# A 160-byte unused tile behind the constants and a decay tile 64 bytes longer: every later tile moves in SBUF

## The chip, the cores and the metric

The kernel runs on one core of one Trainium2 chip. The metric is the device time of one execution in microseconds. Three executions of the kernel before took 225.80 (median), 225.74 and 226.55 us. A profiled execution took 225.21 us, and 223.5 us of it lie between the first and the last instruction of the program (the span). The changes looked at here are small, so every sum below is made against that one profiled execution and then carried over to the median.

## What is computed

The reference has two parts. The first is a Mamba-2 state scan over x (4 batches, 8 heads, 768 steps, 32 channels) with decays a and projections B and C of 16 states, in chunks:

```
log_a = np.log(np.clip(a, 1e-06, 1.0))
...
    cum = np.cumsum(la, axis=-1)
    L = np.exp(cum[:, :, :, None] - cum[:, :, None, :])
...
    M = CB * L
    y_intra = np.einsum('bhij,bhjd->bhid', M, xc)
    decay_to_i = np.exp(cum)
    y_inter = np.einsum('bhin,bhnd->bhid', Cc, state) * decay_to_i[:, :, :, None]
    y[:, :, sl] = y_intra + y_inter
...
    state = decay_full[:, :, None, None] * state + np.sum(Bx, axis=2)
```

The second is a mixer on that result, seen as 4 x 768 tokens of 256 channels: a low-rank mix over the tokens (rank 32), and a two-layer network over the channels (256 to 1024 and back):

```
h = xt @ U @ V
u = x + h.transpose(0, 2, 1)
ch = np.maximum(u @ w_ch1, 0.0) @ w_ch2
return (u + ch).astype(np.float32)
```

Everything is in 32-bit floating point at the interface; four of the weights arrive as 64-bit words and are converted on the chip.

## The kernel before

**Stages.** Each batch is worked in three pairs of 128-step blocks (`pairs`, twelve in all). For a pair the scan loads B, C and x, multiplies in the decays (`prep`, `decayed`), transposes (`turning`), forms the chunk matrices (`gram`, `mask`), updates the states (`state`, `update`) and adds up the output (`inter`, `intra`, `yout`). Then the mixer of that batch does the low-rank part (`project`, `mixed`, `added`) and, for three blocks of 256 tokens, the two layers.

**The two layers.** The first blocks go through `plain`, with 32-bit weights (`w1f`, and `w2f` in tiles named `o`). All other blocks use products in the replicated format FP32R. Each operand is split into a near part, a far part and a joined part, and three products take the place of one. The weights are split once, in `refine`, into the three tiles `w1[0..2]` (printed as w10, w11, w12) and `w2[0..2]`. The inputs of the first layer are split in `split` into three tiles `u0`, `u1`, `u2`; the outputs of the first layer are split in `second` and `third` into tiles named `words`. All products come from the one line in `products` (L772):

```
nc.tensor.matmul(out=t, lhsT=lhsT, rhs=rhs, start=start, stop=True,
                 skip_group_check=True)
```

`lhsT` is the stationary operand (128 columns, 512 B a partition), which a weight load brings in; `rhs` is the moving operand (256 columns, 1024 B a partition). Three uses of it matter here:

- the **up** products (`first` and `second`): stationary w1, moving u; in the profile `x<-u,w` and `z<-u,w`, 480 of them
- the **down** products (`down`): stationary w2, moving words; `x<-words,w` and `z<-words,w`, 432 of them
- the products of **the last block** (`rows`): the roles are exchanged, stationary words, moving w2; `x<-w,words` and `z<-w,words`, 48 of them

**What sets the order.** The order of the work is written out by hand as a list of steps (`PLANS`), and `follow` runs through it; no scheduler moves anything. All instructions of an engine stand in that order. SyncE's queue issues all loads and stores.

**What sets the addresses.** Tiles are laid out in each partition one after the other, pool by pool, each rounded up to 32 B: the pool `const` first (weights, identity, decay constants; the last of it is `settled`, one number), then `raw` (the loads bc and x, and twelve tiles `words`), then `att` (the tiles of the scan: BC, T, Cm, `own`, bd, M, S, Sm, in this order), then `mix` (yT, ytok, pT, o, u0, u1, u2). `own` is a temporary of `keep`, which runs once, at the start, for the decays of the chunks. In the kernel before it has 4 x 11 x 8 numbers, 1408 B.

Of the kernel before, what the change touches and what calls it, by code (L numbers as in the profile page):

```python
# [10 lines left out]
FP32 = mybir.dt.float32  # L11
# [63 lines left out]
def kernel(  # L75
# [28 lines left out]
    P = 128  # L104
    NB, NH, S, D = x.shape
# [13 lines left out]
    Q = 32  # L119
# [3 lines left out]
    const = ctx.enter_context(tc.tile_pool(name="const", bufs=1))  # L123
    raw = ctx.enter_context(tc.tile_pool(name="raw", bufs=4))
    att = ctx.enter_context(tc.tile_pool(name="att", bufs=2))
# [17 lines left out]
    def bank(tag, *dims):  # L143
        t = psum.tile([P, *dims], FP32, tag=tag, name=tag, bufs=BANKS[tag])
        if fills[0]:
            idle(t if len(dims) == 1 else t.rearrange(
                {2: "p a b -> p (a b)", 3: "p a b c -> p (a b c)"}[len(dims)]), fills[0])
        fills[0] = 0
        return t
# [101 lines left out]
    own = {}  # L251
# [124 lines left out]
    def keep(bs, tag="w"):  # L376

        n = bs.stop - bs.start
        d = bank(tag, n, NC, NH)
        nc.tensor.matmul(out=d, lhsT=after, rhs=la[:, bs], start=True, stop=False,  # L380
                         skip_group_check=True)
        nc.tensor.matmul(out=d[:, :, :NC - 1], lhsT=onward, rhs=la[:, bs, 1:], start=False,
                         stop=True, skip_group_check=True)
        nc.scalar.activation(FD[:, bs], d, AF.Exp)

        d = bank(tag, n, NC, 2, NH)
        nc.tensor.matmul(out=d[:, :, :, 0], lhsT=middle, rhs=la[:, bs], start=True, stop=True,
                         skip_group_check=True)
        for m, sl in ((high, slice(0, NC - 1)), (low[0], slice(1, NC))):
            nc.tensor.matmul(out=d[:, :, :NC - 1, 1], lhsT=m, rhs=la[:, bs, sl], start=False,  # L390
                             stop=True, skip_group_check=True)
        J = 2 * NC - 1
        own = att.tile([P, NB, J, NH], FP32, tag="own", name="own", bufs=1)[:, :n]
        vector.tensor_tensor(
            out=own, in0=d.rearrange("p b c v h -> p b (c v) h")[:, :, :J],
            in1=mine[:, None, None, :].to_broadcast(own.shape), op=ALU.mult)
        vector.tensor_reduce(out=kept[:, bs], in_=own, axis=mybir.AxisListType.X, op=ALU.add)
        nc.scalar.activation(kept[:, bs], kept[:, bs], AF.Exp)
# [56 lines left out]

    st = {}
    settled = const.tile([P, 1], FP32)
    behind = {"turn": 0, "first": []}
    yT, ytok = {}, {}

    def prep(k, c=0, n=2):

        b, q = pairs[k]
        if "BC" not in st.setdefault(k, {}):
            st[k]["BC"] = att.tile([P, 2, 2, NH, N], FP32, tag="BC", name="BC")
        for g in [slice(4) if n == 2 else slice(c, c + 1) if c < 2 else slice(2, 4)]:
            part = st[k]["BC"].rearrange("p i c h n -> p (i c) h n")[:, g]
            vector.tensor_tensor(
                out=part, in0=bc_sb[k].rearrange("p h i c n -> p (i c) h n")[:, g],
                in1=F[:, b, q].rearrange("p h i c -> p (i c) h")[:, g, :, None].to_broadcast(  # L470
                    part.shape), op=ALU.mult)
# [479 lines left out]
    def ytokens_of(k, v):  # L951
# [4 lines left out]
                 j=crossed, y=yout, t=ytokens, L=load, Q=lambda k, c: prep(k, c, 1),  # L956
                 E=lambda k, c: decayed(k, c, 1), O=ytokens_of,
                 V=lambda k, c, v: turn(k, c, 1, "wx"[v // 2], vector if v % 2 else None))
    whole = dict(c=convert, R=refined, A=lambda i: decays(every_batch, "w", [i]),
                 K=lambda n: keep(every_batch, "z"), F=fill,  # L960
                 v=lambda n: spread())

# [53 lines left out]
```

## Time and profile before

| | |
|---|---|
| median of three executions | 225.80 us (225.74 to 226.55) |
| profiled execution | 225.21 us |
| its span | 223.5 us |
| granted TensorE clock | 0.999 |
| TensorE matmul busy | 214.7 us, 96% of the span |
| TensorE weight loads busy | 192.8 us, 86% |
| VectorE busy | 163.7 us, 73% |
| ScalarE busy | 122.5 us, 55% |

A matmul's busy time runs from its start to its modelled end and overlaps with the next one, so the time that a matmul costs in a dense stream isn't its duration but the distance from its start to the start of the next. That distance is called the spacing below. In the timeline view, where equal instructions in a row are merged, it can be read as the difference between the starts of two lines divided by the count of the first.

### The profile page before, as it was taken

How to read it: one execution, taken by the hardware profiler on the slowest of the kernel's cores; microseconds unless marked ns; L12 is line 12 of the kernel's file. 1: busy time of each engine (PE TensorE's matmuls, PEld its weight loads, DVE VectorE, ACT ScalarE, POOL GpSimd, SP SyncE). 2: the span in 40 equal slices, each digit the busy share in tenths (PEclk: the TensorE clock that was granted, in tenths of full speed). 3: DMA queues.
4: the chain of work that ended last, by engine and by line, in shares of the span. 5: the costliest groups of instructions: out<-in, count | busy, mean ns of one | idle time of the engine just before them, and what ended most of it. 6: DMA issues, size and time to landing. Idle time of an engine off the chain costs nothing.

```text
span 223.5 us, 7716 instructions
## 1 busy us (share of the span) xinstructions
PE 214.7 (96%) x3374; PEld 192.8 (86%) x3374; DVE 163.7 (73%) x341; ACT 122.5 (55%) x275; POOL 6.5 (3%) x22
## 2 busy tenths in 40 slices
PE   7977899899999999999999999999999999999994
PEld 5846567678889988989999997899998999999994
DVE  3489899999997979688189748948881694917541
ACT  2335774879548655674675351678332357545431
POOL 4023000000000000000000000000000000000000
PEclk9999999999999999999999999999999999999999
DMA  5977899989850005032015010200000000000142
GB/s 86 130 124 130 157 153 229 236 218 154 113 78 4 0 3 94 3 66 81 6 23 73 3 47 3 100 3 1 3 0 3 3 0 0 4 0 0 50 141 94
DMA packets 69345, 14.61 MB, mean 65 GB/s; under 512 B 63616, under 2 KB 67520, under 8 KB 69312
## 3 DMA queue, kind: packets, MB, share of 16 engines
q1 hardware_dynamic: 69312, 14.13, 32.5%
q8 instruction: 26, 0.43, 0.8%
q14 instruction: 7, 0.06, 0.1%
HBM read 10.98 MB, written 3.15 MB: 63 GB/s over the span
## 4 chain that ended last, share of the span: by engine, by line
PE 84%; SPq 8%; DMA 4%; DVE 2%; issue 1%; DVEq 0%
PE x L772 36%; PE z L772 28%; SPq L195 8%; DMA words<-in_moe_w_ch_dram 2%; PE w L730 2%; PE x L652 2%; PE w L891 2%; PE x L527 2%; PE w L701 2%; PE z L676 2%; PE x L741 2%; PE x L676 2%; DMA words<-in_moe_U_dram 1%; PE w L495 1%; PE w L562 1%
## 5 line engine op out<-in xcount | busy, mean ns | idle before, releaser
L169 DVE SCALAR_TENSOR_TENSOR words<-words 128x512 fp32r<-128x512 f32 (+6 forms) x60 | 39.5, 673 | 8.8 <-PE x L772 4.3
L772 PE MATMUL x<-words,w 128*128 128x256 f32 x288 | 39.5, 282 | 0.0
L772 PEld LDWEIGHTS x<-words,w 128*128 128x128 f32 x288 | 35.9, 188 | 1.0 <-issue 0.8
L772 PE MATMUL z<-u,w 128*128 128x256 f32 x240 | 34.4, 282 | 0.0
L772 PE MATMUL x<-u,w 128*128 128x256 f32 x240 | 33.9, 283 | 0.0
L772 PEld LDWEIGHTS z<-u,w 128*128 128x128 f32 x240 | 30.5, 188 | 0.5 <-issue 0.2
L772 PEld LDWEIGHTS x<-u,w 128*128 128x128 f32 x240 | 30.4, 189 | 0.4 <-issue 0.2
L777 ACT ACTIVATE z<-z 128x512 f32<-128x512 f32 (+1 forms) x24 | 13.7, 572 | 15.8 <-PE z L772 15.6
L777 ACT ACTIVATE x<-x 128x512 f32<-128x512 f32 (+1 forms) x27 | 15.3, 572 | 10.4 <-PE x L772 10.3
L772 PE MATMUL z<-words,w 128*128 128x256 f32 x144 | 19.5, 282 | 0.0
L772 PEld LDWEIGHTS z<-words,w 128*128 128x128 f32 x144 | 17.8, 188 | 0.3 <-issue 0.2
L169 DVE SCALAR_TENSOR_TENSOR words<-x,words 128x512 fp32r<-128x512 f32 x20 | 13.7, 686 | 4.8 <-ACT words L812 4.7
L169 DVE SCALAR_TENSOR_TENSOR words<-z,words 128x512 fp32r<-128x512 f32 x20 | 13.7, 686 | 3.1 <-ACT words L812 3.1
L812 ACT ACTIVATE words<-x 128x512 fp32r<-128x512 f32 x20 | 11.9, 600 | 6.5 <-PE x L772 6.5
L812 ACT ACTIVATE words<-z 128x512 fp32r<-128x512 f32 x20 | 11.8, 597 | 5.1 <-PE z L772 5.0
L594 ACT ACTIVATE Sm<-S,slot 128x128 f32<-128x128 f32 (+1 forms) x18 | 6.1, 389 | 14.4 <-DVE S L169 14.4
L169 DVE SCALAR_TENSOR_TENSOR S<-S,kept,w 128x64 f32<-128x64 f32 x40 | 11.2, 280 | 2.5 <-PE w L562 0.8
L169 DVE TENSOR_TENSOR BC<-bc,F 128x512 f32<-128x512 f32 (+2 forms) x18 | 8.7, 509 | 3.2 <-ACT F L372 2.6
L169 DVE TENSOR_TENSOR yT<-x,yT 128x384 f32<-128x384 f32 (+1 forms) x15 | 9.2, 616 | 2.3 <-PE x L772 2.0
L169 DVE TENSOR_TENSOR M<-x,causal 128x256 int32<-128x256 int32 x24 | 9.0, 418 | 2.4 <-PE z L527 2.4
L169 DVE TENSOR_TENSOR u<-yT,u 128x512 fp32r<-128x512 f32 x10 | 6.9, 688 | 5.2 <-ACT u L766 5.2
L652 PE MATMUL z<-T,Sm 32*64 32x64 f32 x180 | 9.7, 236 | 0.3 <-DVE settled L169 0.3
(146 smaller groups left out, 390.6 us busy)
## 6 DMA issues: line engine op xcount, KB each, us to landing
words<-in_moe_w_ch_dram SPq DMA_DIRECT2D x7, 512.0 KB, 6.0
x<-in_x_dram SPq DMA_DIRECT2D x24, 128.0 KB, 3.4
out_dram<-o SPq DMA_DIRECT2D x8, 256.0 KB, 2.2
bc<-in_B_dram SPq DMA_DIRECT2D x24, 64.0 KB, 3.4
bc<-in_C_dram SPq DMA_DIRECT2D x12, 128.0 KB, 3.3
out_dram<-words SPq DMA_DIRECT2D x3, 256.0 KB, 2.6
words<-in_moe_w_ch_dram SPq DMA_DIRECT2D x2, 256.0 KB, 4.5
out_dram<-o SPq DMA_DIRECT2D x2, 128.0 KB, 1.7
```

What stands on the lines that cost most here:

```text
L169: self.last = call(*args, **kwargs)
L195: op = nc.sync.dma_start(**kwargs)
L527: nc.tensor.matmul(out=g[r][cols, c], lhsT=s["T"][rows, 0, c, cols], rhs=s["Cm"][rows, :, :, ts(2 * c + p, Q)].rearrange("r v t i -> r v i ...
L594: nc.scalar.activation(s["Sm"][:, sl, v], s["S"][:, sl, ts(v, D)], AF.Copy, scale=slot[:, v, None])
L652: product = nc.tensor.matmul(out=y[r // 2][p][ts(r % 2, H), c], lhsT=own[ts(r, Q)], rhs=s["T"][ts(r, Q), 1, :, ts(2 * c + p, Q)].rearrange ...
L676: product = nc.tensor.matmul(out=y[n][p][ts(i, Q), c], lhsT=x_sb[k][half, c, h], rhs=s["M"][half, h // 2, c, h % 2], start=fresh(k, n, p, ...
L701: nc.tensor.transpose(out=t[:, c, g], in_=yT[b][:, g, ts(2 * q + c, P)], identity=ident)
L730: nc.tensor.matmul(out=p[ts(q, Q)], lhsT=U_sb[:, c], rhs=ytok[b][:, c, ts(q // 2, P)], start=(c == 0), stop=(c == NC - 1), skip_group_chec ...
L741: nc.tensor.matmul(out=h[q][:, :VS], lhsT=pT[rows], rhs=V4[rows], start=True, stop=True, skip_group_check=True)
L772: nc.tensor.matmul(out=t, lhsT=lhsT, rhs=rhs, start=start, stop=True, skip_group_check=True)
L777: nc.scalar.activation(t, t, AF.Copy, scale=1.0 + EPS)
L812: nc.scalar.activation(gs[j, i][0], t, AF.Relu, scale=NEAR)
```

## The change

A tile `gap` of 40 numbers (160 B) that nothing reads or writes is put behind `settled`, at the end of the pool of constants. The tile `own` becomes 368 numbers long (1472 B instead of 1408), of which the same 352 are used. No instruction is added, taken out or moved, on any engine.

```
@@ keep
         J = 2 * NC - 1
-        own = att.tile([P, NB, J, NH], FP32, tag="own", name="own", bufs=1)[:, :n]
+        own = att.tile([P, 368], FP32, tag="own", name="own", bufs=1)
+        own = own[:, :n * J * NH].rearrange("p (b j h) -> p b j h", b=n, j=J)
         vector.tensor_tensor(
...
     st = {}
     settled = const.tile([P, 1], FP32)
+    gap = const.tile([P, Q + 8], FP32)
```

So the constants stay where they are, the tiles behind them up to `own` move up by 160 B, and the tiles behind `own` by 224 B. The starts in a partition, in bytes, and what is left of them modulo 256:

| tiles | before | after | modulo 256, before | after |
|---|---|---|---|---|
| w10, w11, w12, w20, w21, w22 | 20608 and on, 8192 apart | the same | 128 | 128 |
| w1f, ident | 45184, 77952 | the same | 128 | 128 |
| bc, x, words, BC, T, Cm | words 103104 and on, 4096 apart | 103264 and on | 192 | 96 |
| bd, M, S, Sm, yT, ytok, pT, o, u0, u1, u2 | u0 213056, u1 217152, u2 221248 | u0 213280, u1 217376, u2 221472 | 64 | 32 |

The slices that the products take out of these tiles start at multiples of 256 B in them, so the table holds for every operand. With "distance" for the start of the moving operand less that of the stationary one, modulo 256:

| products | distance before | after |
|---|---|---|
| up (moving u, stationary w1) | -64 | -96 |
| down (moving words, stationary w2) | +64 | -32 |
| the last block (moving w2, stationary words) | -64 | +32 |

More of the change, by code (lines that the diff above doesn't have):

```diff
@@ L392, in keep @@
         J = 2 * NC - 1
-        own = att.tile([P, NB, J, NH], FP32, tag="own", name="own", bufs=1)[:, :n]
+        own = att.tile([P, 368], FP32, tag="own", name="own", bufs=1)
+        own = own[:, :n * J * NH].rearrange("p (b j h) -> p b j h", b=n, j=J)
         vector.tensor_tensor(
@@ L457 @@
     settled = const.tile([P, 1], FP32)
+    gap = const.tile([P, Q + 8], FP32)
     behind = {"turn": 0, "first": []}
```

## The prediction, as it was put on record before the changed kernel ran

> **What bounds the kernel now.** I read the page's first two parts, then the chain that ended last, then the waits of TensorE, and last the matmuls of line L772 in the timeline, since nothing but addresses changes and TensorE's dense stream is where an address could show.
>
> ```profile
> PE 214.7 (96%) x3374; PEld 192.8 (86%) x3374; DVE 163.7 (73%) x341; ACT 122.5 (55%) x275; POOL 6.5 (3%) x22
> ...
> PE   7977899899999999999999999999999999999994
> ...
> PE 84%; SPq 8%; DMA 4%; DVE 2%; issue 1%; DVEq 0%
> ...
> x<-in_x_dram SPq DMA_DIRECT2D x24, 128.0 KB, 3.4
> ...
> bc<-in_C_dram SPq DMA_DIRECT2D x12, 128.0 KB, 3.3
> ```
>
> TensorE's matmuls are 84% of the chain, and from the ninth slice on (45 us) its row has only nines, but for the last; the granted clock is 0.999. The waits of TensorE's matmul rows from 66 us to the end list nothing. The FP32R products begin at 67.4 us and end at 220.2 us. So in that stretch a nanosecond taken from the spacing of the products comes off the time, and one added goes onto it. Before 35 us loads and SyncE's queue lead the chain.
>
> The list of line L772's matmuls gives count and least, median and greatest duration in ns:
>
> ```profile
> L772 PE MATMUL x<-words,w x288: 276/279/388, 83.1 to 211.6; 128*128 128x256 f32 x144
> L772 PE MATMUL z<-u,w x240: 276/281/469, 67.4 to 209.7; 128*128 128x256 f32 x120
> L772 PE MATMUL x<-u,w x240: 276/281/470, 68.6 to 206.9; 128*128 128x256 f32 x120
> L772 PE MATMUL z<-words,w x144: 276/279/393, 119.2 to 213.8; 128*128 128x256 f32 x144
> L772 PE MATMUL x<-yT,w1f x32: 379/379/483, 35.6 to 52.6; 128*128 128x256 f32 x32
> ...
> L772 PE MATMUL x<-w,words x24: 276/276/369, 211.7 to 219.3; 128*128 128x256 f32 x24
> L772 PE MATMUL z<-w,words x24: 276/276/367, 216.2 to 220.2; 128*128 128x256 f32 x24
> ```
>
> All these FP32R products have the same shape. Their least duration is 276 ns everywhere, but the median is 281 for up, 279 for down and 276 for the last block. The timeline of TensorE's matmuls (start, length, operation) shows what this means for the spacing:
>
> ```profile
> 187.38 0.62 PE L772 MATMUL z<-u,w 128*128 128x256 f32 x4
> 187.84 0.62 PE L772 MATMUL x<-u,w 128*128 128x256 f32 x4
> 188.29 0.62 PE L772 MATMUL z<-u,w 128*128 128x256 f32 x4
> 188.74 1.10 PE L772 MATMUL x<-words,w 128*128 128x256 f32 x8
> 189.69 0.63 PE L772 MATMUL x<-u,w 128*128 128x256 f32 x4
> 190.16 1.11 PE L772 MATMUL x<-words,w 128*128 128x256 f32 x8
> 191.10 1.10 PE L772 MATMUL z<-u,w 128*128 128x256 f32 x8
> 192.04 1.11 PE L772 MATMUL x<-u,w 128*128 128x256 f32 x8
> ```
>
> From 187.38 to 188.74, twelve up products take 1.36 us, 113 ns each; from 190.16 to 192.04, sixteen products take 1.88 us, 117.5 each. There are two spacings, and a stream stays in one for many products. I took the starts of all consecutive FP32R matmuls out of the trace and sorted their spacings: up to 115 ns "short" (mean 113.4), 116 to 125 "long" (mean 117.8); some 30 beyond, first ones after another kind of work, are left out.
>
> - down (distance +64): 48 short, 355 long, 12% short
> - up (-64): 169 short, 285 long, 37% short
> - the last block (-64, roles exchanged): 36 short, 5 long, 88% short
> - at distance 0, where one role follows another, two cases: one short, one long
>
> The 646 long ones cost 646 x 4.4 ns = 2.85 us over an all-short stream. The mean over 900 spacings is 116.6 ns.
>
> **The change part by part.** *Instructions.* None is added, removed or moved, so no queue, wait or DMA is passed by another. The whole effect is in how long the same instructions take.
>
> *The down products' distance, +64 to -32.* No run shows -32. Its neighbours are 0 (one of two short) and -64 (37% with u moving, 88% with w2 moving). Bounds: all long, 48 x 4.4 = +0.21 us; all short, 355 x 4.4 = -1.56 us. Both neighbours are better than +64, so I take a gain; I choose the last block's 88% because its operands are the same tiles, words and w2, that the down products use: (0.88 - 0.12) x 403 x 4.4 = -1.35 us. With the up products' 37% it would be -0.44.
>
> *The up products' distance, -64 to -96.* Nothing shows -96; it is one step beyond -64, away from the bad +64. Bounds: all long, 169 x 4.4 = +0.74 us; all short, 285 x 4.4 = -1.25. From 37% I go to 50%, because a down stream that turned short would no longer hand a long rhythm to the up products behind it (at 188.74 a down group turns a short stream long, and it is long at 189.69): 0.13 x 454 x 4.4 = -0.26 us.
>
> *The last block, -64 to +32.* Between 0 and +64: half of its 36 short ones go long, 18 x 4.4 = +0.08 us (bounds -0.02 and +0.16).
>
> *A deeper stall.* The rows don't exclude that a new distance delays each product twice. At 122.2 ns (113.4 + 2 x 4.4; single spacings of 122 occur) the down products would give 355 x 4.4 + 48 x 8.8 = +2.0 us, the up products 285 x 4.4 + 169 x 8.8 = +2.7 us. I take none, and keep these for the range.
>
> *Other products.* The 32-bit ones have spacings of 215 to 216 ns both at -64 (yT, w1f) and at +128 (words, o), hence nothing; were each of the 128 to take 4.4 ns more, +0.56 us. Transposes have 108 to 110 ns at +64 (yT) and at -64 (BC), so nothing. The small products of the scan overlap, several in the array; I take nothing for them.
>
> *Loads.* The 128-byte pieces of C now straddle a multiple of 256 B, which they did not; half of x's 128-byte pieces do so before and after. x's loads land in 3.4 us, C's in 3.3 us: at most 0.1 us a load, and perhaps four of them lead work before 35 us, so 0 to 0.4 us. I take 0.
> [...]
>
> *VectorE and ScalarE.* All tiles behind the constants start at odd multiples of 32 B now, where they were multiples of 64 B. F, an operand of `prep`, already stands so. No row tells the two apart. VectorE's 27% idle time and the absence of TensorE waits after 66 us cover a few ns an instruction; a tenth more on VectorE (16 us) would not be covered and would show as TensorE waits.
>
> Sum: -1.35 - 0.26 + 0.08 = -1.5 us on the profiled 225.21. The median of the runs stands 0.6 us above it, and I put the difference on that: 225.8 - 1.5 = 224.3 us.
>
> **The rivals.** *No change.* The state of a stream would be a matter of chance after each gap, not of the distance. For this: the up products show both states on the same tiles, and both keep themselves going. Against it: 12% short at +64 and 88% in the last block. The counts would be dealt anew, within 0.8 us: 225.8.
> [...] The trace has 113.4 and 117.8 ns for the same shape at full clock, so something does delay these; what, no row here names.
>
> *Slower: the stall becomes steady, or double.* One mechanism: at the new distances the moving stream and the next weight load meet in every product. For it: at +64 this is almost so, and a stream once long stays long. Against it: no group of the trace has a steady spacing over 118. All long at one delay: 254 x 4.4 = +1.1 us, 226.9. Double for one of the two operands: 227.8 (down) or 228.5 (up); for all, 646 x 4.4 + 254 x 8.8 = +5.1, 230.9. It decides when the mean spacing passes 117.8.
>
> *All short.* Both distances lie clear of the stall: -2.85 us, 223.0.
>
> **How the numbers follow.** What a measurement of this kernel can tell from no change is about 0.5%, 1.1 us. Gain by shorter spacings 0.43 (all short 0.13 of it, forecast or near it 0.30); no change 0.25; slower 0.32, 0.13 of it beyond 228.6. Faster thus 0.43, same 0.25, slower 0.32. The likeliest case's own range is 223.0 to 224.7. For 8 in 10, the range goes from 222.9 to 228.6 (one operand doubled), leaving 0.13 above and a few hundredths below.
>
> **What would show it.** In the changed kernel's profile the rows of L772 should have a median near 276 for `words,w`, and 276 to 281 for `u,w`, and sixteen-product lines of down should stand 1.81 us apart instead of 1.88. The prediction is wrong if the medians rise above 281 or the spacing above 118 (a deeper stall), if counts are as before (no influence), or if waits of TensorE or longer VectorE rows turn up after 66 us (the alignment acts elsewhere).

## The result, and the profile after

The changed kernel took 227.95 us (median of ten executions, 226.84 to 229.65), the kernel before 225.69 (median of ten on the same chip, 224.65 to 226.88). The ratio is 1.010, 95% interval 1.007 to 1.013: the change made the kernel 1.0% slower, 2.3 us, where 1.5 us faster had been forecast. The profiled execution after took 227.66 us with a span of 225.9; before it was 225.21 and 223.5.

The page of the changed kernel, first two parts, the chain by engine, and the loads of x and C:

```profile
PE 216.1 (96%) x3374; PEld 193.8 (86%) x3374; DVE 163.8 (72%) x341; ACT 122.7 (54%) x275; POOL 6.5 (3%) x22
...
PE   7978799799999999999999999999999999999994
...
PE 88%; SPq 6%; issue 2%; DMA 1%; DVE 1%; ACT 0%; DVEq 0%
...
x<-in_x_dram SPq DMA_DIRECT2D x24, 128.0 KB, 3.9
...
bc<-in_C_dram SPq DMA_DIRECT2D x12, 128.0 KB, 4.2
```

TensorE still leads the chain. VectorE and ScalarE are busy for as long as before, to 0.2 us. Two things have moved: TensorE's matmuls are busy for 1.4 us more, and the loads land later, x in 3.9 us instead of 3.4 and C in 4.2 instead of 3.3. The matmuls of the line in `products` (L774 now), with least, median and greatest duration in ns:

```profile
L774 PE MATMUL x<-words,w x288: 276/281/388, 83.9 to 213.8; 128*128 128x256 f32 x144
L774 PE MATMUL z<-u,w x240: 277/280/468, 68.2 to 211.9; 128*128 128x256 f32 x120
...
L774 PE MATMUL x<-w,words x24: 277/280/367, 213.9 to 221.7; 128*128 128x256 f32 x24
L774 PE MATMUL z<-w,words x24: 274/280/366, 218.5 to 222.6; 128*128 128x256 f32 x24
```

The median of down went from 279 to 280 or 281, and that of the last block from 276 to 280. That of up is 1 ns lower than before and yet up has become slower, because a median says nothing of a mixture; the spacing does. The first FP32R product starts at 68.2 us instead of 67.4. In the timeline of the same kernel (start, length, operation) the long streams look like this:

```profile
192.22 1.11 PE L774 MATMUL x<-words,w 128*128 128x256 f32 x8
193.17 1.11 PE L774 MATMUL z<-u,w 128*128 128x256 f32 x8
194.12 1.11 PE L774 MATMUL x<-u,w 128*128 128x256 f32 x8
195.06 1.11 PE L774 MATMUL z<-u,w 128*128 128x256 f32 x8
196.02 1.58 PE L774 MATMUL x<-u,w 128*128 128x256 f32 x12
```

Sixteen products of up from 193.17 to 195.06 take 1.89 us, 118 ns each. One by one the spacings of up run through 115, 117, 119, 122, 120 and start again: no longer two rhythms, one of 113 and one of 118, but a single one that swings between 115 and 122. No spacing of up is 113 or 114 any more; there were 165 before. The means of the ordinary spacings (up to 126 ns; the products that come first after other work lie beyond), from the starts of all consecutive FP32R matmuls:

| products | before: distance, mean | after: distance, mean | difference |
|---|---|---|---|
| down | +64, 117.4 ns | -32, 118.2 ns | 404 x 0.9 = +0.36 us |
| up | -64, 116.1 ns | -96, 118.0 ns | 453 x 1.8 = +0.82 us |
| the last block | -64, 114.0 ns | +32, 117.0 ns | 42 x 3.0 = +0.12 us |

That is 1.3 us. With the 0.8 us by which the first FP32R product starts later, 2.1 of the 2.4 us between the two spans are accounted for. The other 0.3 us are a single wait of TensorE, in front of one small product of the scan at 144.3 us; it is the only one that the list of TensorE's waits after 66 us has (what it waited for: us in total, times, longest). For the kernel before the same list is empty:

```profile
PE z L654 <- issue: 0.3, 1, 0.3
```

A wait of 0.2 to 0.6 us in front of such a product, between 142 and 146 us, is in eight of the fourteen profiles of this case, with changed distances and with those of before. It goes neither with a distance nor with the place of the loads, and its cause is open.

### The profile page after: what moved, and what is told of

Its sections match the earlier page's. It is cut to its first block, busy times and chain, and to the rows that moved or that the text cites. A ratio compares the mean times of both kernels' runs of the same rounds, so it can differ in the third digit from the quotient of the medians.

```text
span 225.9 us, 7716 instructions
## 1 busy us (share of the span) xinstructions
PE 216.1 (96%) x3374; PEld 193.8 (86%) x3374; DVE 163.8 (72%) x341; ACT 122.7 (54%) x275; POOL 6.5 (3%) x22
## 4 chain that ended last, share of the span: by engine, by line
PE 88%; SPq 6%; issue 2%; DMA 1%; DVE 1%; ACT 0%; DVEq 0%
PE x L774 36%; PE z L774 28%; SPq L195 6%; PE x L654 3%; PE w L732 3%; PE x L529 2%; PE w L893 2%; PE z L678 2%; PE w L703 2%; PE x L678 2%; PE w L497 2%; PE x L743 1%; PE w L564 1%; DMA words<-in_moe_U_dram 1%; PE z L654 1%
## 5 line engine op out<-in xcount | busy, mean ns | idle before, releaser
L774 PE MATMUL x<-words,w 128*128 128x256 f32 x288 | 39.7, 284 | 0.0
L774 PEld LDWEIGHTS x<-words,w 128*128 128x128 f32 x288 | 36.1, 188 | 1.0 <-issue 0.8
L774 PE MATMUL z<-u,w 128*128 128x256 f32 x240 | 34.9, 284 | 0.0
L774 PE MATMUL x<-u,w 128*128 128x256 f32 x240 | 34.2, 284 | 0.0
L774 PEld LDWEIGHTS z<-u,w 128*128 128x128 f32 x240 | 30.8, 188 | 0.5 <-issue 0.2
L774 PEld LDWEIGHTS x<-u,w 128*128 128x128 f32 x240 | 30.6, 188 | 0.4 <-issue 0.2
L774 PE MATMUL z<-words,w 128*128 128x256 f32 x144 | 19.7, 283 | 0.0
L774 PEld LDWEIGHTS z<-words,w 128*128 128x128 f32 x144 | 18.0, 188 | 0.3 <-issue 0.2
```

## The experiments

Two explanations stood against each other and against chance. **A**: the distance between the moving operand and the weights, modulo 256, sets the rhythm of the FP32R products. **B**: the loads of bc and x have become slower, because their pieces now lie differently against multiples of 256 or 64 B. **C**: any move of the addresses deals the rhythm anew.

All experiments only place unused bytes: behind `settled` (as in the change), in `own`, or between x and words, where `load_v` makes a tile `skip` before the first tile `words` is made. So bc and x, words, and u can be moved apart from each other. In the diffs below, the second line that `own` needs (its rearrangement, as in the change) is left out.

One thing has to be known to read the profiles. Many executions, of the kernel before too, have a mean granted clock of 0.96 to 0.98 instead of nearly 1. In the nine profiles of this sort the clock is at about half for a while between 17 and 35 us, as in this row of the control below:

```profile
PEclk9995589999999999999999999999999999999999
```

The profiles of before, of the changed kernel and of three others (the down products alone, distance -64 for both, loads on multiples of 256 B) have no such dip. The start of the first FP32R product is therefore compared only with executions of the same sort, and the spacing after it is free of the dip. Even so that start scatters: with the loads standing as before it lies at 67.4 and 67.7 us without the dip and at 68.4 to 69.2 us with it. A difference of 0.8 us between two profiles is rough, and the ratios say more of the loads.

**The control: everything moves by 256 B.**

```
     settled = const.tile([P, 1], FP32)
+    gap = const.tile([P, 64], FP32)
```

> The unused tile is 256 B, the decay tile as before: every tile behind the constants moves, but all remainders modulo 256 and all distances are those of before. Theory A (the distance between the moving operand and the weights, modulo 256, sets the spacing of the FP32R products): mean spacing 116.6 ns as before, short ones about 12% in down, 37% in up; time within 0.5 us of before. Theory B (the loads of bc and x have become slower because their pieces lie differently against multiples of 256 or 64 B): no change either, x and C land in 3.3 to 3.4 us. Theory C (any move of the addresses deals the rhythm anew): spacing and time differ from before by up to 1 us either way.

Ratio 0.999 (0.996 to 1.002). Down 117.7, up 116.0, the last block 114.0 ns; C lands in 3.2 us. Moving by itself does nothing to the time, and explanation C falls. The counts are not fixed, though: over the six kernels with all the distances of before, down has 4 to 12% short spacings and up 29 to 44%; the control has 4% and 41%.

**The down products alone.**

```
+    gap = const.tile([P, 40], FP32)
...
-        own = att.tile([P, NB, J, NH], FP32, tag="own", name="own", bufs=1)[:, :n]
+        own = att.tile([P, 376], FP32, tag="own", name="own", bufs=1)
```

> Unused tile of 160 B, decay tile longer by 96 B: words and the loads of bc and x stand as in the changed kernel, u and everything behind the decay tile as before. Distances: down -32, up -64, the last block +32. Theory A: down 118.2 ns and the last block 117.0 as in the changed kernel, up near 116.1 as before, unless the long rhythm is handed over from down to up (then up to 117.5); in all +0.5 to +1.1 us. Theory B: the first FP32R product starts 0.8 us late (68.2 us instead of 67.4) and C lands in 4.2 us; after that no loss; +0.8 us. A and B together +1.3 to +1.9.

Ratio 1.0055 (1.003 to 1.008). Down 118.1 and the last block 117.0 ns as in the changed kernel, up 116.1 as before; C lands in 4.3 us, and the first FP32R product starts at 68.6 us, in an execution without the dip. Both A and B show, each at its place; together, 1.2 us by the ratio, they are just under the 1.3 to 1.9 that was expected.

**The up products alone.**

```
-        own = att.tile([P, NB, J, NH], FP32, tag="own", name="own", bufs=1)[:, :n]
+        own = att.tile([P, 408], FP32, tag="own", name="own", bufs=1)
```

> No unused tile, decay tile longer by 224 B: u and everything behind the decay tile stand as in the changed kernel, words and the loads of bc and x as before. Distances: up -96, down +64, the last block -64. Theory A: up near 118.0 ns, no spacing of 113 in it, +0.8 us; down 117.4 or, if no short rhythm is left to be handed over, 117.9 (+0.2). Theory B: the first FP32R product starts at 67.4 us, C lands in 3.3 us, no loss at all.

Ratio 1.003 (1.000 to 1.006). Up 117.8 ns with four spacings of 114 and none of 113; down 117.5; C lands in 3.2 us. A again. The last block went from 114.0 to 116.8 ns although its distance is that of before; it begins with a long rhythm here and keeps it longer. Why is open.

**The loads alone.**

```
+    gap = const.tile([P, 40], FP32)
...
+        raw.tile([P, 24], FP32, tag="skip", name="skip", bufs=1)
```

> Unused tile of 160 B, and a second one of 96 B between x and words: only bc and x stand as in the changed kernel, all other tiles have the remainders of before. Distances as before. Theory A: spacing as before (116.6 ns), no loss. Theory B: C lands in about 4.2 us, x in 3.9, the first FP32R product starts at about 68.2 us, the whole is 0.8 us slower.

Ratio 1.005 (1.002 to 1.008). The spacing is that of before (116.4 ns over all), and C lands in 4.2 us. B is real as well: about 1.1 us (0.4 to 1.8) with nothing else changed. The line of the load queue (packets, MB, share of the 16 engines' span), of this kernel and of the control:

```profile
q1 hardware_dynamic: 69312, 14.13, 33.0%
```

```profile
q1 hardware_dynamic: 69312, 14.13, 32.1%
```

The same packets and bytes take 0.9 points more of the span.

**Distance, or where the operands stand?** All distances after the change are odd multiples of 32 B. Here everything, the weights too, moves by 32 B, and the distances stay.

```
+    ahead = const.tile([P, 8], FP32)
     a_sb = const.tile([NB * NH * NC // 2, 2, P], FP32)
...
+    gap = const.tile([P, 56], FP32)
...
+        raw.tile([P, 8], FP32, tag="skip", name="skip", bufs=1)
```

> A tile of 32 B ahead of the constants, so weights, words and u all move by 32 B modulo 256 (weights 160, words 224, u 96), with pads that keep bc and x at their remainder of before: distances up -64, down +64, the last block -64, as before, but every operand at an odd multiple of 32 B. If the distance alone decides: means as before, up near 116, down 117.4, the last block 114, with many spacings of 113. If the operands' own alignment decides (odd multiples of 32 B lose the short state): no 113 left, up and down near 118.

Down 117.6, up 116.3, the last block 114.0 ns, with 112 spacings of 113 and 114 in up (one profiled execution; the spacings alone are read). It is the distance, not the operand's own place.

**Which boundary slows the loads?**

```
+    gap = const.tile([P, 32], FP32)
...
+        raw.tile([P, 32], FP32, tag="skip", name="skip", bufs=1)
```

> Two pads of 128 B: bc and x start at 64 modulo 256, a multiple of 64 B, all other remainders as before. The 128-byte pieces of C straddle a multiple of 256 B (they did not before), B's pieces don't, x's do in half of the cases, as before. If the straddling of 256 B is what slows the loads: C lands in about 4.2 us, and the time is up to 0.5% longer than before, as with the loads moved by 160 B. If odd multiples of 32 B are (every piece then straddles a multiple of 64 B): C lands in 3.2 to 3.3 us, and the time is as before, within 0.3%.

Ratio 1.005 (1.002 to 1.008), at a start that is a multiple of 64 B; spacing 116.6 ns as before. The loads on this page:

```profile
x<-in_x_dram SPq DMA_DIRECT2D x24, 128.0 KB, 3.8
...
bc<-in_C_dram SPq DMA_DIRECT2D x12, 128.0 KB, 4.0
```

So odd multiples of 32 B are not needed for it. What this kernel and those with the loads at 96 modulo 256 share, and the kernel before doesn't have, is that C's pieces straddle a multiple of 256 B. Over all kernels C lands in 3.1 to 3.5 us without straddling and in 4.0 to 4.3 with it.

**Distance 0.**

```
-        own = att.tile([P, NB, J, NH], FP32, tag="own", name="own", bufs=1)[:, :n]
+        own = att.tile([P, 384], FP32, tag="own", name="own", bufs=1)
...
+        raw.tile([P, 48], FP32, tag="skip", name="skip", bufs=1)
```

> bc and x as before; words and u both at 128 modulo 256: distance 0 for up, down and the last block. If distances that are multiples of 64 B keep the short state: part of the spacings at 113, mean 114 to 117.4, time from 1.0% faster to 0.3% slower. If the operands meeting at the same remainder is the worst case: all long or over, mean over 118, 0.5% slower or more.

Ratio 1.014 (1.011 to 1.017). The spacing is 119.8 ns for up and down and 119.6 for the last block, and 785 of the 900 ordinary spacings are 120. The matmuls of this kernel:

```profile
L774 PE MATMUL x<-words,w x288: 278/283/387, 84.6 to 215.4; 128*128 128x256 f32 x144
L774 PE MATMUL z<-u,w x240: 278/283/467, 68.8 to 213.6; 128*128 128x256 f32 x120
```

This is a steady stall, as the slower rival has it, with the operands starting at the same remainder; its size lies between that rival's single delay (117.8) and double delay (122.2). The 32-bit products (`yT,w1f` and `words,o`), which stand at distance 0 here too, keep their spacing of 215 to 216 ns, so in this kernel they don't show the effect.

**Distance -64 for both.**

```
-        own = att.tile([P, NB, J, NH], FP32, tag="own", name="own", bufs=1)[:, :n]
+        own = att.tile([P, 384], FP32, tag="own", name="own", bufs=1)
...
+        raw.tile([P, 32], FP32, tag="skip", name="skip", bufs=1)
```

> bc and x as before; words and u both at 64 modulo 256: distance -64 for up and down, +64 for the last block. If the distance decides, whatever the role: down becomes like up, 40% short, mean 116.1 instead of 117.4; the last block becomes like down was (117.4 instead of 114.0); up stays at 116 or gets better, as no long rhythm is handed over. In all 0.4 to 1.0 us faster, 0.2 to 0.45%. If the role matters (words against w2): down stays at 117.4, no gain.

Ratio 0.994 (0.992 to 0.997): 0.56% faster than before, a little more than the 0.2 to 0.45% expected. Down 115.0 ns with 64% short ones, where 40% had been expected, up 115.3 with 58%; the last block, now at +64, 117.8. Words behave like u at the same distance, so the role makes no difference between these two, and +64 is a long place for w2 against words too. The list of this kernel's matmuls and a piece of its timeline:

```profile
L774 PE MATMUL x<-words,w x288: 276/276/388, 83.3 to 210.6; 128*128 128x256 f32 x144
L774 PE MATMUL z<-u,w x240: 276/278/471, 67.7 to 208.7; 128*128 128x256 f32 x120
```

```profile
154.29 0.62 PE L774 MATMUL x<-u,w 128*128 128x256 f32 x4
154.75 1.98 PE L774 MATMUL x<-words,w 128*128 128x256 f32 x16
156.56 1.07 PE L774 MATMUL x<-u,w 128*128 128x256 f32 x8
```

From 154.75 to 156.56 sixteen down products take 1.81 us, 113 ns each: the rhythm that the prediction had hoped for at -32. It is not handed back and forth any more between up and down; one stretch keeps it for 101 products. Yet here, too, a long rhythm can last, in one stretch over 241 products.

**Loads on multiples of 256 B.**

```
+    gap = const.tile([P, 16], FP32)
...
+        raw.tile([P, 48], FP32, tag="skip", name="skip", bufs=1)
```

> Pads of 64 B behind the constants and 192 B between x and words: bc and x start at 0 modulo 256, all other remainders and all distances as before. No 128-byte piece of C or x straddles a multiple of 256 B any more; before, half of x's did (12,288 pieces), in the kernels with slower loads these and all of C's (24,576). If a straddling piece costs its share: x lands below 3.4 us, and the time falls by about what C's straddling added, 0.3 to 0.5%. If only C's loads stand in the way of other work: no change, within 0.2%.

Ratio 1.001 (0.998 to 1.004), x in 3.3 us, C in 3.2. No gain: that half of x's pieces straddled a multiple of 256 B before had cost nothing that can be measured, though the kernels in which C's straddle as well (96 and 64 modulo 256, distances as before) take 0.5% longer. In the profiled execution the first FP32R product starts at 65.9 us, 1.5 us before that of the kernel before, but the runs together show nothing of it.

The records of single packets say more. The pieces of C and x are 36,864 packets of 128 B. In the kernel before, 98.7% of them take at most 13 ns; with the loads alone moved it is still 93.3%, and with the loads at 64 it is 96.1%, though C's straddling pieces are a third of all. So most pieces that straddle take no longer than others; a few take far longer, up to 299 and 314 ns against 65. Straddling alone isn't the whole of B: why only some packets are drawn out, and what tells C's loads from x's, is open.

**Both together.**

```
-        own = att.tile([P, NB, J, NH], FP32, tag="own", name="own", bufs=1)[:, :n]
+        own = att.tile([P, 384], FP32, tag="own", name="own", bufs=1)
...
+    gap = const.tile([P, 16], FP32)
...
+        raw.tile([P, 16], FP32, tag="skip", name="skip", bufs=1)
```

> Both together: bc and x at 0 modulo 256, words and u at 64, distances -64 for up and down. If the two effects add up: 0.56% from the distances and 0.3 to 0.5% from the loads, 0.9 to 1.1% faster than before; mean spacing 115.2 to 115.5 ns. If the earlier end of the loads is eaten by waits elsewhere: 0.5 to 0.6% faster.

Ratio 0.997 (0.993 to 1.001), mean spacing 115.5 ns. The two don't add up to more, as the previous run lets one expect; the interval reaches over no change and over the 0.56% of the distances alone. The ratio is also blurred by the clock: of the executions compared, 5 of 12 of this kernel and 4 of 19 of the kernel before have a mean granted clock of 0.97 or less. Within that group this kernel is 0.6% faster, within the rest 0.2%. So a gain beyond that of the distances isn't seen, and whether some of theirs is lost stays open.

**Two more distances.**

```
-        own = att.tile([P, NB, J, NH], FP32, tag="own", name="own", bufs=1)[:, :n]
+        own = att.tile([P, 392], FP32, tag="own", name="own", bufs=1)
...
+        raw.tile([P, 8], FP32, tag="skip", name="skip", bufs=1)
```

> bc and x as before; u at 0, words at 224 modulo 256: distance 128 for up, +96 for down, -96 for the last block. Two more points of the spacing against the distance. If odd multiples of 32 B have no lasting short state: down near 118 with a mix of 115 to 122 and no run of 113; the last block 117 to 118. Distance 128, the farthest from the worst one (0, where up took 119.8): if the spacing falls with the way from 0, up below 115.3; if -64 is a place of its own, 117 to 118.

Down at +96 119.5 ns, up at 128 118.7, the last block at -96 118.7 (one profiled execution). Being far from 0 doesn't help; -64 is a place of its own. All distances that were seen, by mean spacing:

| distance | mean spacing, ns | where |
|---|---|---|
| -96 | 117.8 to 118.1 (last block, one kernel, 118.7) | up, three kernels |
| -64 | 114.9 to 116.5 (last block 114.0 to 116.8) | up and down, nine kernels |
| -32 | 118.1 to 118.2 | down, three kernels |
| 0 | 119.8 (last block 119.6) | all, one kernel |
| +32 | 117.0 | the last block, three kernels |
| +64 | 117.4 to 117.9 | down, the last block, nine kernels |
| +96 | 119.5 | down, one kernel |
| 128 | 118.7 (118.9 with nine of 128 to 129 ns that the limit of 126 leaves out) | up, one kernel |

**The changed distances without the moved loads.**

```
-        own = att.tile([P, NB, J, NH], FP32, tag="own", name="own", bufs=1)[:, :n]
+        own = att.tile([P, 368], FP32, tag="own", name="own", bufs=1)
...
+        raw.tile([P, 40], FP32, tag="skip", name="skip", bufs=1)
```

> The decay tile of 1472 B as in the changed kernel, but the 160 B stand between x and words instead of behind the constants: words 96, u 32 modulo 256 and all distances (-96, -32, +32) as in the changed kernel, bc and x as before. If distances and loads are two separate parts of the changed kernel's 1.0%: spacing 118.0 ns as there, C lands in 3.1 to 3.4 us, and 0.45 to 0.65% slower than before. If the distances alone make the 1.0%: 0.9 to 1.1% slower.

Ratio 1.007 (1.004 to 1.010), spacing 118.1 ns, C in 3.4 us. The ratio is a little over what was expected of the distances alone, and its interval just reaches the 1.0% of the whole change. From the start of the first FP32R product to that of the last there is no wait for a load and no dip. Less the one wait near 144 us where there is one, this kernel needs 154.1 us for that stretch and the changed one 154.1; the six kernels with the distances of before need 152.7 to 152.9. So the distances are worth 1.2 to 1.5 us, as the table of the spacings has it (1.3). The loads and that one wait make up the rest of the 2.3.

## Why the prediction was wrong

- **What bounds the kernel** was right: TensorE's dense stream leads (88% of the chain after), and what was added to the spacing, 1.3 us, came onto the time.
- **The down products' distance, +64 to -32** is the step that failed first. It took -1.35 us; the spacing changed by +0.36 us. The value for -32 was drawn between its neighbours at 0 and -64, as if the spacing were a smooth function of the distance, and then taken from the better of them. It isn't smooth: 119.8 at 0, 118.1 at -32, 114.9 to 116.5 at -64, 118 again at -96. The neighbour at 0, of which before had two cases, one of them short, is the worst of the eight places seen; two single spacings, at the seams between streams, did not tell what a stream at that distance does.
- **The up products' distance, -64 to -96** failed in sign by the same reasoning: -0.26 us taken, +0.82 measured, and its upper bound (+0.74, all at the long spacing of 118) was just passed, since the new rhythm swings up to 122.
- **The last block** came near: +0.08 taken, +0.12 measured, though most of its short spacings went, not half of them (37 of 42 spacings were short before, 7 are after).
- **Loads** were sized wrong: 0 taken, at most 0.4 bounded; the first FP32R product started 0.8 us later, and the loads moved alone cost 1.1 us. The bound came from x's landing time, of whose pieces half straddle; C's whole load does, and it landed 0.9 us later, not 0.1.
- **The rival that came nearest** is the slower one: the stall becomes steady. Its price for one delay everywhere, +1.1 us, is near the 1.3 us of the three rows of the spacing table, and its point of decision, a mean over 117.8, was passed at 118.0. But the spacing of up and down isn't a steady 117.8 after the change; it swings between 115 and 122. The double stall (122.2 throughout) was not seen at any distance. That the moving stream and the next weight load meet, as this rival has it, was the author's guess: the runs show that the spacing goes with the distance between the two operands, not what delays a product.
- **The range**, 222.9 to 228.6 us, holds the measured 227.95, but by luck: its upper end stood for one operand with a double stall. What brought the time there was a single stall's worth of spacing and the loads, which the sum had at nothing.
- **The signs of being wrong**: the medians of up and down, 280 and 281, did not rise above 281, but the mean spacing passed 118. The one wait of 0.3 us after 66 us is no sign of another effect of the alignment, since other kernels with other distances have it too.
- **The rival "no change"** fell with the control, the move by 32 B and the distances 0 and -64: rhythm and distance belong together. What chance leaves at one distance is small (116.4 to 116.9 ns over six kernels). The same instructions take 119.8 ns at distance 0 and 115.0 to 115.3 at -64.

## What to carry to other kernels

In this kernel's dense stream of FP32R products, each with its own weight load, the place of the moving tile against the weights, modulo 256 B, was worth a few per cent of each product (115 to 120 ns), and tiles that are only padded moved it. In another such stream it is worth a measurement, at the very distance: here two known points said nothing of the ones between. Pads that move one group of tiles also move those behind it; check what happens to the loads, and use a pad of 256 B as control.

## What had not been expected of the hardware

- Of eight distances in steps of 32 B, -64 often has a lasting rhythm of 113 ns and +64 seldom, the others none (+32 was seen only on the 42 spacings of the last block); at 0 the products lock to 120 (785 of 900 spacings). The 32-bit products keep 215 to 216 ns at distance 0 too.
- A stream keeps its rhythm over long stretches at the same distance, 101 products at 113 and 241 at 118 in one kernel; the mixture, not the single product, is what the distance changes.
- C's loads, in 128-byte pieces, took 4.0 to 4.3 us instead of 3.1 to 3.5 when every piece lay across a multiple of 256 B, and x's landed later too (3.7 to 4.0 us instead of 3.3 to 3.6). That cost 0.5% of the whole. Over 87% of the packets took their usual 13 ns all the same; a few took up to 0.3 us.
